# The second dense product of a retention and feed-forward kernel, from block 2 on, as Strassen's seven products of quarters

## The chip, the cores and the metric

One core of a Trainium2 chip. The metric is the device time of one execution, in microseconds. The kernel's engines are named as the profile names them: PE (TensorE), DVE (VectorE), ACT (ScalarE), POOL (GpSimd) and SP (SyncE, which issues most transfers here).

## The reference

Inputs are `q`, `k`, `v` of 4 batches x 8 heads x 768 steps x 64, `w_in` 512 x 2048, `w_out` 2048 x 512 and `alpha` of 2048, all float32. A retention recurrence gives 3072 rows of 512, and a feed-forward block with a leaky activation follows:

```python
for t in range(S):
    state = gamma[None, :, None, None] * state + np.einsum('bhd,bhe->bhde', k[:, :, t], v[:, :, t])
    y[:, :, t] = scale * np.einsum('bhd,bhde->bhe', q[:, :, t], state)
...
x = y.transpose(0, 2, 1, 3).reshape(B * S, H * D)        # 3072 x 512
h = x @ w_in                                             # 3072 x 2048
g = np.maximum(h, 0.0) + alpha * np.minimum(h, 0.0)
out = g @ w_out                                          # 3072 x 512
```

## The kernel before

The 3072 rows are worked in six blocks of 512 (`NBLK`, numbered 0 to 5). Everything that TensorE reads is float16, its sums are float32 in PSUM. Each block has three kinds of work.

**Retention.** A block's rows are four units of 128 steps (`u0` to `u0 + 3`). `load` (line 114) brings a unit's k, q and v in, on SP's queue. `prep` has GpSimd scale k, then q by a table (`scaled`, line 125, two operations), has SP issue a transposing transfer of both (line 146), and has GpSimd cast v (line 140). In pairs of units, `scores` (line 220) and `states` (line 180) are small matmuls of 64 x 64. VectorE then forms the running states (`sums`, lines 195 to 201, with one step on GpSimd, line 203) and masks the scores (`masked`, line 234). `outputs` (line 254) multiplies masked scores and states, and ScalarE copies the result to `xT` (line 302), which the next block's first dense product reads. The first two blocks do this in double units (names that begin with `u`, lines 317 to 520), which the change does not touch.

**First dense product, `ffn1`.** Sixteen tiles `ft` of 128 hidden columns, each 4 matmuls of 128 x 128 weights by 512 columns (line 538) into one of four PSUM banks (`tag="pb"`). ScalarE takes the rectified negative `hm` (line 547, three buffers), and VectorE joins both into the tile `gt[:, ft, :]` (line 548, one operand in SBUF, one in PSUM). `ffn1_half` (lines 569 to 583) does the same with 256 columns, for block 0 alone.

**Second dense product, `ffn2`.** For each of four row groups of 128, sixteen matmuls with a piece of `gt` as weights and 512 columns of `w_out` (line 607). ScalarE copies the bank to `os` (line 616) and issues its store (line 620).

The order is written out by hand: each engine works its instructions in the order in which the program issues them. The products are generators, and `tick(gen, m)` issues the next `m` of their matmuls, so that the retention's steps lie between them. In blocks 1 to 4 the next block's units run between the matmuls of the second product, and their scaling is issued within the first:

```python
gen = ffn2(n)
if more:
    for i in range(0, UB, 2):
        us = [u0 + i, u0 + i + 1]
        pq = scores(us)
        states(us)
        sums(us[0])
        masked(us, pq)
        sums(us[1])
        tick(gen, 22)
        outputs(us)
        tick(gen, 8)
```

The last block has no such units beside it.

Of the kernel before, what the change touches and what calls it, by code (L numbers as in the profile page):

```python
# [9 lines left out]
FP = mybir.dt.float32  # L10
F16 = mybir.dt.float16
COPY = mybir.ActivationFunctionType.Copy
RELU = mybir.ActivationFunctionType.Relu
MULT = mybir.AluOpType.mult
ADD = mybir.AluOpType.add


@with_exitstack
def kernel(
# [10 lines left out]
    nc = tc.nc  # L30
    B, H, S, D = q.shape
    d_model, d_ff = moe_w_in.shape
    NFT = d_ff // 128
# [4 lines left out]
    UB = 4  # L38
    NBLK = NU // UB
    TB = UB * C  # L40
    scale = 1.0 / np.sqrt(D)
# [63 lines left out]
    def load(u):  # L105
        b, c = divmod(u, NCH)
        kq_ = ring(f"kqs{u}")
        if u % 2 == 0:
            vpair[u] = vpair[u + 1] = ring(f"vs{u}")
        v_ = vpair.pop(u)[:, 512 * (u % 2) : 512 * (u % 2) + 512]  # L110
        t = {"k": kq_[:, 0:512], "q": kq_[:, 512:1024], "v": v_}
        for nm, src in (("k", k), ("q", q), ("v", v)):
            t[nm] = t[nm].rearrange("p (h d) -> p h d", d=D)
            nc.sync.dma_start(
                out=t[nm],
                in_=src[b, :, C * c : C * c + C, :].rearrange("h p d -> p h d"),
            )
        staged[u] = t
# [92 lines left out]
    def scores(us, again=0):  # L211
        sc = [ps("sca"), ps("scb")]
        for _ in range(again):
            nc.tensor.matmul(out=sc[0], lhsT=ident, rhs=wz, start=True, stop=True)
        for t, u in enumerate(us):
            for i in range(4):
                at = 64 * (4 * t + i)
                for r in range(2):
                    for X in range(2):
                        nc.tensor.matmul(  # L220
                            out=sc[r][HALF[X], at : at + 64],
                            lhsT=kqT[u][HALF[r], i, HALF[X]],
                            rhs=kqT[u][HALF[r], 4 + i, HALF[X]],
                            start=True,
                            stop=True,
                        )
        return sc

    def masked(us, sc):
        m2s[us[0]] = []  # L230
        n = 4 * len(us)
        for r in range(2):
            m2 = sbp.tile([128, 8, 64], F16, tag=f"m2{r}", bufs=2, name=f"m2{r}")
            nc.vector.tensor_tensor(
                out=m2[:, 0:n, :],
                in0=sc[r][:, 0 : 64 * n].rearrange("p (a j) -> p a j", j=64),
                in1=mask.unsqueeze(1).to_broadcast([128, n, 64]),
                op=MULT,
            )
            m2s[us[0]].append(m2)  # L240
# [287 lines left out]

    gts = {}

    def ffn1(n, lo=0):
        if n not in gts:
            gts[n] = sbp.tile([128, NFT, TB], F16, tag="gt", bufs=2, name=f"gt{n}")
        gt = gts[n]
        for ft in range(lo, NFT):
            hps = ps("hps", tag="pb")
            for hp in range(4):
                nc.tensor.matmul(  # L538
                    out=hps,
                    lhsT=w_in_all[:, hp, 128 * ft : 128 * ft + 128],  # L540
                    rhs=xT[n][:, :, hp, :],
                    start=(hp == 0),
                    stop=(hp == 3),
                )
                if hp == 3:
                    hm = sbp.tile([128, TB], FP, tag="hm", bufs=3, name="hm")
                    nc.scalar.activation(out=hm, in_=hps, func=RELU, bias=0.0, scale=-1.0)  # L547
                    nc.vector.scalar_tensor_tensor(  # L548
                        out=gt[:, ft, :],
                        in0=hm,  # L550
                        scalar=oma_sb[:, ft : ft + 1],
                        in1=hps,
                        op0=MULT,
                        op1=ADD,
                    )
                yield

    def ffn1_half(n, half, lo=0, hi=NFT, again=0, late=None):
        if n not in gts:
            gts[n] = sbp.tile([128, NFT, TB], F16, tag="gt", bufs=2, name=f"gt{n}")  # L560
        gt = gts[n]
        to = slice(256 * half, 256 * half + 256)
        for f0 in range(lo, hi, 2):
            hps = ps("hps", tag="pb")
            for _ in range(again if f0 == lo else 0):
                nc.tensor.matmul(out=hps, lhsT=ident, rhs=wz, start=True, stop=True)
            for ft in (f0, f0 + 1):
                for hp in range(4):
                    nc.tensor.matmul(  # L569
                        out=hps[:, 256 * (ft - f0) : 256 * (ft - f0) + 256],  # L570
                        lhsT=w_in_all[:, hp, 128 * ft : 128 * ft + 128],
                        rhs=xT[n][:, half, hp, :],
                        start=(hp == 0),
                        stop=(hp == 3),
                    )
                    if ft > f0 and hp == 3:
                        hm = sbp.tile([128, TB], FP, tag="hm", bufs=3, name="hm")
                        nc.scalar.activation(out=hm, in_=hps, func=RELU, bias=0.0, scale=-1.0)

                        def prelu(f0=f0, hm=hm, hps=hps):  # L580
                            for f in (f0, f0 + 1):
                                at = slice(256 * (f - f0), 256 * (f - f0) + 256)
                                nc.vector.scalar_tensor_tensor(  # L583
                                    out=gt[:, f, to],
                                    in0=hm[:, at],
                                    scalar=oma_sb[:, f : f + 1],
                                    in1=hps[:, at],
                                    op0=MULT,
                                    op1=ADD,
                                )  # L590

                        if late is None:
                            prelu()
                        else:
                            late.append(prelu)
                    yield

    def ffn2(n, parts=1):
        gt = gts.pop(n)
        opss = {}  # L600
        step = NFT // parts
        for f0 in range(0, NFT, step):
            for tq in range(UB):
                if f0 == 0:
                    opss[tq] = ps("ops", tag="pb")
                for ft in range(f0, f0 + step):
                    nc.tensor.matmul(  # L607
                        out=opss[tq],
                        lhsT=gt[:, ft, 128 * tq : 128 * tq + 128],
                        rhs=w_out_all[:, ft, :],  # L610
                        start=(ft == 0),
                        stop=(ft == NFT - 1),
                    )
                    if ft == NFT - 1:
                        os_sb = sbp.tile([128, d_model], FP, tag="os", bufs=4, name="os")
                        nc.scalar.activation(  # L616
                            out=os_sb, in_=opss[tq], func=COPY, bias=0.0, scale=1.0
                        )
                        row = TB * n + 128 * tq
                        (nc.scalar if n else nc.sync).dma_start(out=out[row : row + 128, :], in_=os_sb)  # L620
                    yield


    def flush(late):
        while late:
# [2 lines left out]
    def tick(gen, m):  # L628
        for _ in range(m):
            if next(gen, 1) == 1:  # L630
                return
# [171 lines left out]
    gen = ffn1(1)  # L803
# [7 lines left out]
    prep(11)  # L811
    load(14)
    load(15)
    for _ in gen:
        pass

    for n in range(1, NBLK):
        more = n + 1 < NBLK
        u0 = UB * (n + 1)
        if n > 1:  # L820
            gen = ffn1(n)
            if more:
                for i in range(UB):
                    tick(gen, 14)
                    prep(u0 + i)
                    if u0 + i + UB < NU:
                        load(u0 + i + UB)
            for _ in gen:
                pass
        gen = ffn2(n)  # L830
        if more:
            for i in range(0, UB, 2):
                us = [u0 + i, u0 + i + 1]
                pq = scores(us)
                states(us)
                sums(us[0])
                masked(us, pq)
                sums(us[1])
                tick(gen, 22)
                outputs(us)  # L840
                tick(gen, 8)
        for _ in gen:
            pass


# [28 lines left out]
```

## Time and profile before

| | |
|---|---|
| median of 3 runs | 214.5 us (214.11 to 214.72) |
| the profiled execution | 213.28 us, of which the span of the core's instructions is 211.5 us |
| busy in the span | PE 202.4, DVE 116.5, ACT 95.5, POOL 75.2 us |
| line 607 (second product) | 384 matmuls |
| line 538 (first product, whole blocks) | 352 matmuls |
| transfers | 27.44 MB read, 6.29 MB written |

How to read the rows that follow. In the groups by line, a row names line, engine, operation, output and inputs, the shape, how often it ran, then its busy time in us with the mean of one in ns, and behind the second bar the idle time of the engine just ahead of it with what ended most of it. In the timeline a row begins with the start and the length in us; equal instructions that follow each other are one row with their count. In the chain of waits, the work that ended last is followed back from the end; a row is start, length and the engine and line that held the chain. PE's matmuls are pipelined, so one's duration is longer than the distance between two; `PEclk` is the clock that was granted, in tenths.

### The profile page before, as it was taken

The page shows a single profiled execution, that of the slowest core. Times are in us where ns is not written, and L with a number is a line of the kernel's source. Part 1 is how long each engine was busy: PE and PEld are TensorE (multiplying, and loading weights), DVE is VectorE, ACT ScalarE, POOL GpSimd, SP SyncE. Part 2 cuts the span into 40 slices and gives each one's busy share as a digit, 9 for nine tenths or more (in the row PEclk, how much of TensorE's full clock was granted, in tenths as well). Part 3 has the DMA queues.
Part 4 walks back from the last instruction along what each step waited for, and adds up shares of the span by engine and source line. Part 5 has one row for each costly group of instructions (what it writes and reads, how often), then busy time and mean ns, then how long its engine had stood idle before and what let it go on. Part 6 is the DMA issues. An engine that isn't in the chain of part 4 may idle for free.

```text
span 211.5 us, 5579 instructions
## 1 busy us (share of the span) xinstructions
PE 202.4 (96%) x2355; PEld 100.6 (48%) x2355; DVE 116.5 (55%) x193; ACT 95.5 (45%) x160; POOL 75.2 (36%) x106
## 2 busy tenths in 40 slices
PE   7779999999999999999999999999999999999993
PEld 3544855454444554444454444444444444444441
DVE  2676997565288722288722388531488540588000
ACT  2334575353766232566233566133566133665121
POOL 0336899348830209900207930118920210000000
PEclk9999999999999999999999999999999999999999
DMA  6999999999999999999512999813660111100112
GB/s 181 332 333 359 394 376 337 319 297 218 249 271 241 193 262 212 276 219 224 134 53 99 237 203 226 194 52 113 159 69 0 52 55 50 50 3 0 50 70 79
DMA packets 87688, 38.27 MB, mean 181 GB/s; under 512 B 68064, under 2 KB 80496, under 8 KB 87664
## 3 DMA queue, kind: packets, MB, share of 16 engines
q1 hardware_dynamic: 84464, 32.60, 61.5%
q10 hardware_dynamic: 3200, 5.33, 7.0%
q8 instruction: 18, 0.29, 0.6%
q14 instruction: 6, 0.05, 0.1%
HBM read 27.44 MB, written 6.29 MB: 159 GB/s over the span
## 4 chain that ended last, share of the span: by engine, by line
PE 89%; DMA 5%; DVE 2%; issue 1%; SPq 1%; ACT 0%; DVEq 0%
PE ops L607 40%; PE hps L538 36%; DMA ku<-in_k_dram 3%; PE hps L569 3%; PE ya L254 2%; DMA qu<-in_q_dram 2%; DVE ukq L331 1%; PE sca L220 1%; PE trb L360 1%; PE ya L462 1%; PE sca L439 1%; PE yb L254 1%; SPq L317 1%; PE sta L180 1%; PE sta L374 1%
## 5 line engine op out<-in xcount | busy, mean ns | idle before, releaser
L548 DVE SCALAR_TENSOR_TENSOR gt<-hm,oma,hps 128x512 f16<-128x512 f32 x88 | 65.4, 747 | 42.9 <-ACT hm L547 33.9
L607 PE MATMUL ops<-wout,gt 128*128 128x512 f16 x384 | 87.7, 380 | 0.0
L538 PE MATMUL hps<-xT,win 128*128 128x512 f16 x352 | 77.0, 379 | 0.0
L547 ACT ACTIVATE hm<-hps 128x512 f32<-128x512 f32 x88 | 52.5, 597 | 23.5 <-PE hps L538 23.0
L607 PEld LDWEIGHTS <-gt 128*128 128x128 f16 x384 | 35.6, 98 | 40.4
L538 PEld LDWEIGHTS <-win 128*128 128x128 f16 x352 | 34.4, 98 | 41.4 <-issue 0.2
L616 ACT ACTIVATE os<-ops 128x512 f32<-128x512 f32 x24 | 14.3, 597 | 54.2 <-PE ops L607 54.1
L203 POOL TENSOR_TENSOR t<-ss,tab 128x256 f16<-128x256 f32 x13 | 8.0, 612 | 74.7 <-DVE ss L201 74.7
L125 POOL TENSOR_TENSOR kq<-kqs,tab 128x512 f16<-128x512 f32 x32 | 32.7, 1041 | 1.7 <-DMA kqs<-in_k_dram 1.7
L195 DVE TENSOR_TENSOR t<-t,sta 128x256 f16<-128x256 f16 x13 | 5.4, 412 | 14.5 <-PE stb L180 14.5
L673 POOL CAST wout<-wo 128x512 f16<-128x512 f32 x14 | 8.3, 613 | 6.7 <-DMA wo<-in_moe_w_out_dram 6.3
L302 ACT ACTIVATE xT<-ya 128x512 f16<-128x512 f32 x8 | 4.8, 597 | 11.6 <-PE yb L254 11.6
L140 POOL CAST vx<-vs 128x512 f16<-128x512 f32 x16 | 9.7, 609 | 0.0
L673 POOL CAST win<-wi 128x512 f16<-128x512 f32 x14 | 8.2, 613 | 3.0 <-DMA wi<-in_moe_w_in_dram 3.0
L369 ACT ACTIVATE ukT<-trb 128x512 f16<-128x512 f16 (+1 forms) x8 | 5.6, 704 | 6.7 <-PE trb L360 6.7
L569 PE MATMUL hps<-xT,win 128*128 128x256 f16 x64 | 7.5, 273 | 0.4 <-ACT xT L520 0.4
L450 DVE TENSOR_TENSOR um<-sca,mi 128x512 f16<-128x512 f32 x8 | 5.5, 687 | 3.5 <-PE scb L439 3.5
L569 PEld LDWEIGHTS <-win 128*128 128x128 f16 x64 | 6.1, 98 | 1.6 <-issue 0.8
L360 PE MATMUL trb<-mi,ukq 128*128 128x128 f16 x64 | 4.9, 220 | 1.8 <-DVE ukq L331 1.8
L346 POOL CAST uv<-vu 128x512 f16<-128x512 f32 x6 | 3.6, 612 | 8.3 <-DMA vu<-in_v_dram 8.2
L583 DVE SCALAR_TENSOR_TENSOR gt<-hm,oma,hps 128x256 f16<-128x256 f32 x16 | 6.3, 472 | 0.0
L201 DVE TENSOR_TENSOR ss<-t,stb 128x256 f32<-128x256 f16 x13 | 5.5, 421 | 1.0
(72 smaller groups left out, 145.3 us busy)
## 6 DMA issues: line engine op xcount, KB each, us to landing
out_dram<-os ACTq DMA_DIRECT2D x20, 256.0 KB, 2.0
wo<-in_moe_w_out_dram SPq DMA_DIRECT2D x8, 512.0 KB, 8.3
kqs<-in_k_dram SPq DMA_DIRECT2D x16, 256.0 KB, 3.9
kqs<-in_q_dram SPq DMA_DIRECT2D x16, 256.0 KB, 4.3
vs<-in_v_dram SPq DMA_DIRECT2D x16, 256.0 KB, 4.5
wi<-in_moe_w_in_dram SPq DMA_DIRECT2D x6, 512.0 KB, 7.7
ku<-in_k_dram SPq DMA_DIRECT2D x3, 512.0 KB, 7.2
vu<-in_v_dram SPq DMA_DIRECT2D x3, 512.0 KB, 7.6
```

Of the source, the lines that this page charges most:

```text
L125: eng.tensor_tensor(out=kqs[u][:, a].rearrange("p i r d -> p r i d"), in0=staged[u][nm].rearrange("p (r i) d -> p r i d", i=4), in1=tab[:, ...
L140: eng.tensor_copy(out=vs16[u], in_=staged[u]["v"])
L203: nc.gpsimd.tensor_tensor(out=t0, in0=ss, in1=tab[:, 2 * H : 2 * H + 4].unsqueeze(2).to_broadcast([128, 4, 64]), op=MULT,)
L254: ins = nc.tensor.matmul(out=yv[X][HALF[c], hp, t, :], lhsT=lhsT, rhs=rhs, start=(X, c) not in fresh, stop=last, skip_group_check=True,)
L360: nc.tensor.transpose(out=trv[:, i - i0, :, j, :], in_=ukq[w][:, a, j, i].rearrange("p r d -> p (r d)"), identity=ident,)
L538: nc.tensor.matmul(out=hps, lhsT=w_in_all[:, hp, 128 * ft : 128 * ft + 128], rhs=xT[n][:, :, hp, :], start=(hp == 0), stop=(hp == 3),)
L547: nc.scalar.activation(out=hm, in_=hps, func=RELU, bias=0.0, scale=-1.0)
L548: nc.vector.scalar_tensor_tensor(out=gt[:, ft, :], in0=hm, scalar=oma_sb[:, ft : ft + 1], in1=hps, op0=MULT, op1=ADD,)
L569: nc.tensor.matmul(out=hps[:, 256 * (ft - f0) : 256 * (ft - f0) + 256], lhsT=w_in_all[:, hp, 128 * ft : 128 * ft + 128], rhs=xT[n][:, half ...
L607: nc.tensor.matmul(out=opss[tq], lhsT=gt[:, ft, 128 * tq : 128 * tq + 128], rhs=w_out_all[:, ft, :], start=(ft == 0), stop=(ft == NFT - 1),)
L616: nc.scalar.activation(out=os_sb, in_=opss[tq], func=COPY, bias=0.0, scale=1.0)
L673: eng.tensor_copy(out=to, in_=t)
```

## The change

From block 2 on, the second product's operands are taken as 2 x 2 quarters: rows in two halves of 256, hidden columns in two halves of eight tiles (`HF`), output columns in two halves of 256. Instead of eight products of quarters there are seven, of sums of quarters, in the arrangement with shared sums.

- `w_sums` forms four sums of quarters of `w_out` (128 x 2048 each): two on GpSimd behind block 1's last `prep`, two on VectorE within block 1's second product.
- `g_sums` forms four sums of quarters of `gt`, each in two parts of 128 x 1024 (part 0: hidden tiles 0 to 3 and 8 to 11, part 1: the others). Sum 1 needs sum 0, and sum 3 needs sum 1. VectorE forms sums 0 and 1, GpSimd sums 2 and 3. The first parts of sums 0, 1 and 2 are issued within the first product, behind its tenth tile; on GpSimd that stands between the `prep` of the second and of the third unit. The others are issued at the end of the first product or, on GpSimd, between the steps of `sums`.
- `ffn1` takes its tiles in the order 0, 8, 1, 9, ..., 7, 15.
- `seven` issues 7 x 16 matmuls of 256 columns into four banks. Products that belong together add up in a bank; ScalarE copies a bank three times in between (`kept`), VectorE adds bank and copy to `os` (`put`, four times), and ScalarE issues the store of a quarter, 256 rows of 256 columns. The last quarter's store is issued behind two tiles of the next first product.
- Scores and states of the first pair of units now stand ahead of the last sums; `tick` counts are 40 and 16 instead of 22 and 8.
- `gt` has one buffer instead of two.

```diff
-    def ffn1(n, lo=0):
+    def ffn1(n, lo=0, fts=None):
...
-            gts[n] = sbp.tile([128, NFT, TB], F16, tag="gt", bufs=2, name=f"gt{n}")
+            gts[n] = sbp.tile([128, NFT, TB], F16, tag="gt", bufs=1, name=f"gt{n}")
...
-        for ft in range(lo, NFT):
+        for ft in fts or range(lo, NFT):
...
+    def minus(eng, out, a, b, op=SUB):
+        eng.tensor_tensor(out=out, in0=a, in1=b, op=op)
...
+        f = slice(4 * part, 4 * part + 4)
+        f8 = slice(HF + 4 * part, HF + 4 * part + 4)
+        t0, t1 = slice(0, 256), slice(256, 512)
+        if which == 0:
+            minus(eng, sm[0][:, f], gt[:, f, t1], gt[:, f8, t1], op=ADD)
+        elif which == 1:
+            minus(eng, sm[1][:, f], sm[0][:, f], gt[:, f, t0])
+        elif which == 2:
+            minus(eng, sm[2][:, f], gt[:, f, t0], gt[:, f, t1])
+        else:
+            minus(eng, sm[3][:, f], gt[:, f8, t0], sm[1][:, f])
...
+        def product(bank, a, w, first=False):
+            for t in range(2):
+                for f in range(HF):
+                    nc.tensor.matmul(
+                        out=bank[:, 256 * t : 256 * t + 256],
+                        lhsT=a[:, f, 128 * t : 128 * t + 128],
+                        rhs=w[:, f, :],
...
+        b, a = ps("ops", tag="pb"), ps("ops", tag="pb")
+        yield from product(b, A(0, 0), W(0, 0), True)
+        s1 = kept(b, "um0")
+        yield from product(a, A(0, 1), W(1, 0), True)
+        store = put(0, 0, a, s1)
+        yield from product(b, sm[1], wsum[1])
+        u2 = kept(b, "um0")
+        store()
+        c = ps("ops", tag="pb")
+        yield from product(c, sm[0], wsum[0], True)
+        yield from product(b, sm[2], wsum[2])
+        u3 = kept(b, "um1")
+        store = put(1, 1, c, u3)
+        d = ps("ops", tag="pb")
+        yield from product(d, A(1, 1), wsum[3], True)
+        store()
+        store = put(1, 0, u3, d, SUB)
+        yield from product(c, sm[3], W(1, 1))
+        store()
+        late_stores.append(put(0, 1, c, u2))
...
+            gen = ffn1(n, fts=[HF * (f % 2) + f // 2 for f in range(NFT)])
+            tick(gen, 8)
+            flush(late_stores)
+            tick(gen, 6)
+            for i in range(UB):
+                if more:
                     prep(u0 + i)
                     if u0 + i + UB < NU:
                         load(u0 + i + UB)
+                tick(gen, 14)
+                if i == 1:
+                    g_sums(n, 0, 0, nc.vector)
+                    g_sums(n, 0, 1, nc.vector)
+                    g_sums(n, 0, 2, nc.gpsimd)
...
+            if more:
+                us = [u0, u0 + 1]
+                pq = scores(us)
+                states(us)
+            g_sums(n, 1, 0, nc.vector)
+            g_sums(n, 1, 1, nc.vector)
+            pend = [(1, 2), (0, 3), (1, 3)]
...
+        pool_sum(1 if more else 3)
+        gen = seven(n) if quick else ffn2(n)
```

More of the change, by code (lines that the diff above doesn't have):

```diff
@@ L15 @@
 ADD = mybir.AluOpType.add
+SUB = mybir.AluOpType.subtract
 @with_exitstack
@@ L559, in ffn1_half @@
         if n not in gts:
-            gts[n] = sbp.tile([128, NFT, TB], F16, tag="gt", bufs=2, name=f"gt{n}")
+            gts[n] = sbp.tile([128, NFT, TB], F16, tag="gt", bufs=1, name=f"gt{n}")
         gt = gts[n]
@@ L621, in ffn2, with w_sums @@
                     yield
+    HF = NFT // 2
+    gsum, wsum = {}, {}
+    def minus(eng, out, a, b, op=SUB):
+        eng.tensor_tensor(out=out, in0=a, in1=b, op=op)
+    def w_sums(which, eng):
+        b = [[w_out_all[:, HF * j : HF * j + HF, 256 * l : 256 * l + 256] for l in range(2)] for j in range(2)]
+        i = which
+        wsum[i] = sbp.tile([128, HF, 256], F16, tag=("ukq", "ukT")[i // 2], bufs=2, name=f"wsum{i}")
+        x, y = (
+            (lambda: (b[0][1], b[0][0])),
+            (lambda: (b[1][1], wsum[0])),
+            (lambda: (b[1][1], b[0][1])),
+            (lambda: (wsum[1], b[1][0])),
+        )[i]()
+        minus(eng, wsum[i], x, y)
@@ new lines, in g_sums @@
+    def g_sums(n, part, which, eng):
+        if n not in gsum:
+            gsum[n] = [
+                sbp.tile([128, HF, 256], F16, tag=f"gs{i}", bufs=1, name=f"gs{n}{i}") for i in range(4)
+            ]
+        gt, sm = gts[n], gsum[n]
+        f = slice(4 * part, 4 * part + 4)
[9 more added lines that the diff above has]
+            minus(eng, sm[3][:, f], gt[:, f8, t0], sm[1][:, f])
@@ new lines, in seven, with A, W, kept @@
+    def seven(n):
+        gt, sm = gts.pop(n), gsum.pop(n)
+        def product(bank, a, w, first=False):
[5 more added lines that the diff above has]
+                        rhs=w[:, f, :],
+                        start=first and t == 0 and f == 0,
+                        stop=(f == HF - 1),
+                        skip_group_check=True,
+                    )
+                    yield
+        def A(i, j):
+            return gt[:, HF * j : HF * j + HF, 256 * i : 256 * i + 256]
+        def W(j, l):
+            return w_out_all[:, HF * j : HF * j + HF, 256 * l : 256 * l + 256]
+        def kept(bank, tag):
+            t = sbp.tile([128, 512], FP, tag=tag, bufs=2, name="kept")
+            nc.scalar.activation(out=t, in_=bank, func=COPY, bias=0.0, scale=1.0)
+            return t
+        def put(i, l, x, y, op=ADD):
+            os_sb = sbp.tile([128, d_model], FP, tag="os", bufs=4, name="os")
+            nc.vector.tensor_tensor(out=os_sb, in0=x, in1=y, op=op)
+            row = TB * n + 256 * i
+            return lambda: nc.scalar.dma_start(
+                out=out[row : row + 256, 256 * l : 256 * l + 256].rearrange(
+                    "(t p) c -> p t c", p=128
+                ),
+                in_=os_sb.rearrange("p (t c) -> p t c", t=2),
+            )
+        b, a = ps("ops", tag="pb"), ps("ops", tag="pb")
[18 more added lines that the diff above has]
+        late_stores.append(put(0, 1, c, u2))
@@ L624, in flush @@
+    late_stores = []
     def flush(late):
@@ L813 @@
     load(15)
+    w_sums(0, G)
+    w_sums(2, G)
     for _ in gen:
@@ L819 @@
         u0 = UB * (n + 1)
+        quick = n > 1
         if n > 1:
[L821 to L824, printed above, removed]
+            gen = ffn1(n, fts=[HF * (f % 2) + f // 2 for f in range(NFT)])
[4 more added lines that the diff above has]
+                if more:
                     prep(u0 + i)
@@ L827, with pool_sum @@
                         load(u0 + i + UB)
+                tick(gen, 14)
[3 more added lines that the diff above has]
+                    g_sums(n, 0, 2, nc.gpsimd)
             for _ in gen:
                 pass
-        gen = ffn2(n)
+        pend = []
+        if quick:
+            if more:
[5 more added lines that the diff above has]
+            pend = [(1, 2), (0, 3), (1, 3)]
+        def pool_sum(m=1):
+            for p, w in pend[:m]:
+                g_sums(n, p, w, nc.gpsimd)
+            del pend[:m]
+        pool_sum(1 if more else 3)
+        gen = seven(n) if quick else ffn2(n)
         if more:
@@ L833 @@
                 us = [u0 + i, u0 + i + 1]
-                pq = scores(us)
-                states(us)
+                if i or not quick:
+                    pq = scores(us)
+                    states(us)
                 sums(us[0])
+                pool_sum()
                 masked(us, pq)
                 sums(us[1])
-                tick(gen, 22)
+                pool_sum()
+                tick(gen, 40 if quick else 22)
+                if n == 1:
+                    w_sums(1 + i, nc.vector)
                 outputs(us)
-                tick(gen, 8)
+                tick(gen, 16 if quick else 8)
         for _ in gen:
             pass
+    flush(late_stores)
 _INS = ['q', 'k', 'v', 'moe_w_in', 'moe_w_out', 'moe_alpha']
```

## The prediction

> **What bounds the kernel now.** I read the page's busy line and clock row first, then the chain of waits, then the timeline of one block.
>
> ```profile
> PE 202.4 (96%) x2355; PEld 100.6 (48%) x2355; DVE 116.5 (55%) x193; ACT 95.5 (45%) x160; POOL 75.2 (36%) x106
> PEclk9999999999999999999999999999999999999999
> PE 89%; DMA 5%; DVE 2%; issue 1%; SPq 1%; ACT 0%; DVEq 0%
> ```
> ```profile
> 22.42 5.35 PE hps L569 x48
> ...
> 117.75 13.81 PE hps L538 x64
> 131.56 0.15 PE sca L220 x2
> 132.21 4.86 PE ops L607 x22
> ...
> 149.00 13.81 PE hps L538 x64
> ...
> 194.04 13.83 PE ops L607 x64
> 207.89 0.60 ACT os L616
> ```
>
> From block 2 on TensorE never waits: 64 matmuls of 512 columns take 13.81 us in the first product and 13.83 in the second, 216 ns each at full clock, and a block takes 149.00 - 117.75 = 31.25 us. So a matmul saved is time saved, and any wait put ahead of TensorE is time added.
>
> **The products.** Per block 64 matmuls of 512 columns (13.83 us) become 7 x 16 = 112 of 256 columns. The only such matmuls before are line 569's.
>
> ```profile
> 22.35 5.42 PE L569 MATMUL hps<-xT,win 128*128 128x256 f16 x48
> ```
>
> The last one's pipelined 0.27 us taken off, (5.42 - 0.27)/47 = 109.5 ns each, so 112 x 0.1095 = 12.27: 1.56 us saved per block. The chain's 5.35/48 = 111.5 ns would leave 1.35; both loaded new weights for every matmul, as the seven products do. A page of the Trainium skill speaks against the change here: "TensorE: Matmul & The Clock Gate", section Back-to-back issue gap, gives sustained spacings of about 81 ns at 128 columns and 131 ns at 512. A straight line between them, my estimate, is 98 ns at 256, and 112 x 0.098 - 64 x 0.131 would be 2.6 us lost per block. The rows above disagree (216 and 109.5 ns), so it gets no chance.
>
> **What the sums cost alone.** A part of a sum is 128x1024, all 16-bit and in SBUF. Before has no such VectorE operation; the nearest rows:
>
> ```profile
> L548 DVE SCALAR_TENSOR_TENSOR gt<-hm,oma,hps 128x512 f16<-128x512 f32 x88 | 65.4, 747 | 42.9 <-ACT hm L547 33.9
> L234 DVE TENSOR_TENSOR m<-sca,mi 128x512 f16<-128x512 f32 x8 | 5.5, 683 | 0.0
> L367 DVE COPY ukT<-trb 128x512 f16<-128x512 f16 x6 | 2.5, 423 | 3.4 <-PE trb L360 3.4
> L201 DVE TENSOR_TENSOR ss<-t,stb 128x256 f32<-128x256 f16 x13 | 5.5, 421 | 1.0
> L125 POOL TENSOR_TENSOR kq<-kqs,tab 128x512 f16<-128x512 f32 x32 | 32.7, 1041 | 1.7 <-DMA kqs<-in_k_dram 1.7
> L203 POOL TENSOR_TENSOR t<-ss,tab 128x256 f16<-128x256 f32 x13 | 8.0, 612 | 74.7 <-DVE ss L201 74.7
> ```
>
> Lines 201 and 234 give (683 - 421)/256 = 1.02 ns per element, so 683 + 512 x 1.02 = 1.2 us at worst. The all-16-bit copy does 512 in 423 ns, about half per element: 0.423 + 512 x 0.52 ns = 0.69 us. I take 0.69, since every operand is 16-bit as in the copy, and keep 1.2. GpSimd: lines 203 and 125 give 1.68 ns per element, so 1.9 us a part.
>
> The weights' sums (twice the size: two on GpSimd, 1.04 + 1536 x 1.68 ns = 3.6 us each, two on VectorE in block 1) cost nothing: GpSimd has 11.04 us idle ahead of block 1's second product, and VectorE waits out the rest of its stage.
>
> ```profile
> 71.23 0.61 POOL L203 TENSOR_TENSOR t<-ss,tab 128x256 f16<-128x256 f32 x1 [11.04 <-DVE ss L201]
> ```
>
> **What the sums cost together.** VectorE and GpSimd work at the same time with two SBUF inputs each only once before:
>
> ```profile
> 15.16 0.68 DVE L331 TENSOR_TENSOR ukq<-qu,tab 128x512 f16<-128x512 f32 x1
> 15.33 0.99 POOL L413 TENSOR_TENSOR ut<-uss,tab 128x256 f16<-128x256 f32 x1 [3.27 <-DVE uss L411]
> 15.77 1.10 DVE L331 TENSOR_TENSOR ukq<-qu,tab 128x512 f16<-128x512 f32 x1
> ```
> ```profile
> L413 POOL TENSOR_TENSOR ut<-uss,tab x3: 612/613/991, 15.3 to 50.8; 128x256 f16<-128x256 f32 x3
> ```
>
> GpSimd's operation takes 0.99 instead of 0.61: it runs after VectorE's first has ended (15.84). VectorE's second takes 1.10 instead of 0.68: it ends 0.55 us after GpSimd's end (16.32). They take turns, whole operations at a time; line 548 (one SBUF tensor, one PSUM) keeps its 0.75 beside a busy GpSimd. The Trainium skill, "SBUF — State Buffer", section SBUF: two separate sides, states this as a rule: a VectorE operation with two SBUF inputs and a GpSimd one exclude each other for a whole instruction, and who starts first holds. By that rule, the trace agrees; without turns the sum would be that of the first rival. Bounds for a wait of VectorE: 0, or the rest of a GpSimd operation (up to 1.04 us behind line 125, 1.9 behind a part of a sum). I take turns.
>
> **First half of the sums, inside the first product.** Times count from its first matmul, 117.59.
>
> ```profile
> 117.59 13.98 PE L538 MATMUL hps<-xT,win 128*128 128x512 f16 x64
> 118.86 1.26 ACT L547 ACTIVATE hm<-hps 128x512 f32<-128x512 f32 x2 [0.47 <-PE hps L538]
> 119.49 13.49 DVE L548 SCALAR_TENSOR_TENSOR gt<-hm,oma,hps 128x512 f16<-128x512 f32 x16 [7.15 <-ACT hm L547]
> 129.68 1.89 PE L538 MATMUL hps<-xT,win 128*128 128x512 f16 x8
> 23.08 6.34 DVE L583 SCALAR_TENSOR_TENSOR gt<-hm,oma,hps 128x256 f16<-128x256 f32 x16
> L583 DVE SCALAR_TENSOR_TENSOR gt<-hm,oma,hps 128x256 f16<-128x256 f32 x16 | 6.3, 472 | 0.0
> ```
>
> Tile i (0 to 15) of gt starts on VectorE at 1.90 + 0.863 i and takes 0.75; without a wait VectorE does one each 0.67 us (line 583's sixteen: (6.34 - 0.47)/15 = 0.39, that is 0.08 under one's duration). GpSimd, queued between the units' scalings, does sum 2 when tile 6 is there, 7.9 to 9.8, then unit u0+2's k (to 10.84) and q. VectorE's sum 0 is due behind tile 9, at 10.34: it waits for k, ends 11.4. q was waiting and holds to 12.4; sum 1, which needs sum 0, ends 12.9. Tile 10 then starts at 12.9 instead of 10.53 and ends 13.65. Tile 14's matmuls, due at 129.68 - 117.59 = 12.09, write the PSUM bank that tile 10 empties (four banks in turn), and start at 13.7: **1.6 us lost**. SP's order is unchanged, but its last two transposes of units follow GpSimd some 6 us later; they are needed some 5 us after they land, so nothing is lost.
>
> **Second half, at the seam.** Tile 14: matmul 13.7, ScalarE 14.97 to 15.57, gt at 16.35; tile 15 ends 17.2. GpSimd's sum 2, freed by tile 14, holds 16.4 to 18.3. VectorE's sum 0 is due at 17.1, ends 18.85; sum 1 ends 19.65. Queued behind them are the state sums and masks, for which the unit's outputs wait:
>
> ```profile
> 132.90 0.41 DVE L195 TENSOR_TENSOR t<-t,sta 128x256 f16<-128x256 f16 x1
> 133.41 0.42 DVE L201 TENSOR_TENSOR ss<-t,stb 128x256 f32<-128x256 f16 x1
> 133.75 0.68 DVE L234 TENSOR_TENSOR m<-sca,mi 128x512 f16<-128x512 f32 x1
> 134.35 0.68 DVE L234 TENSOR_TENSOR m<-scb,mi 128x512 f16<-128x512 f32 x1
> 134.95 0.41 DVE L195 TENSOR_TENSOR t<-t,sta 128x256 f16<-128x256 f16 x1
> 136.99 0.22 PE L254 MATMUL ya<-m,vx 64*64 64x64 f16 x2
> 137.26 0.20 PE L254 MATMUL ya<-kt,t 64*64 64x64 f16 x2
> ```
>
> Before, they end 135.36, 1.9 us ahead of their last use (137.26). Now they take the same 2.46 us from 19.6: 22.05. TensorE ends the first product at 15.4, scores and states take 0.65, and 40 matmuls of 109.5 ns bring the outputs to 20.45 and that last use to 20.7: **1.4 us lost**. The second pair of units, with nothing beside it, waits for nothing. A middle block (2, 3, 4): -1.56 + 1.6 + 1.4 = +1.44; three: +4.3.
>
> **Last block.** No scalings, so sum 0 and 1 run 10.34 to 11.8, tile 10 ends 12.5: 0.45 lost. No scores either: product 1 starts at 14.26 and its eighth matmul (15.03) waits for tile 14 (15.2): 0.25. GpSimd's sum 2 holds 15.25 to 17.15, VectorE's sum 0 then ends 17.7, GpSimd's waiting sum 3 holds to 19.6, sum 1 ends 20.15; product 3's fifth matmul, due at 18.45, needs it: 1.75. Product 7 waits for copy and addition behind product 5, about 0.1. Together -1.56 + 2.55 = +1.0.
>
> **Stores.**
>
> ```profile
> 207.89 0.60 ACT L616 ACTIVATE os<-ops 128x512 f32<-128x512 f32 x1 [2.86 <-PE ops L607]
> 208.52 0.34 ACTq L620 DMA_DIRECT2D out_dram<-os  x1
> out_dram<-os ACTq DMA_DIRECT2D x20, 256.0 KB, 2.0
> kqs<-in_k_dram SPq DMA_DIRECT2D x16, 256.0 KB, 3.9
> ```
>
> As many stores, in 1 KB rows instead of 2 KB; only the last shows. An addition (line 234's 0.68) replaces a copy of 0.60, and ScalarE's queue must hear of it: +0.2. Landing lies between 2.0 and the 3.9 of the 256-byte loads, so 0 to 1.9 more; I take 0, nearer to the store.
>
> **Sum.** 4.3 + 1.0 + 0.2 = +5.5. The profiled execution took 213.28 (span 211.5 and 1.8 around it): 218.8. The runs' median, 214.5, is 1.2 above it: **220.0 us**.
>
> **Rivals.**
> - *The engines don't take turns* (the one overlap is special: line 413's first call). Then a middle block loses 0.45 in the first product, as the last block does, and about 0.35 at the outputs: -0.76. The last: -0.76. Sum 4 x -0.76 + 0.2 = -2.8: **211.6**. For it: one event only. Against: both sides of it fit turns to 0.1 us.
> - *Turns in one place only*, for instance GpSimd reaches unit u0+2 later than tile 9 or gives way faster: 3 x 1.2 less than forecast and below, **213 to 217**.
> - *Sums at 1.2 us.* Half a microsecond more in each of four steps in a row: a middle block loses 2.7 + 2.4, the last 4.7: 3 x 3.5 + 3.1 + 0.2 = +13.8: **228**. For it: no two-input 16-bit row in before; against: line 367.
> - *GpSimd keeps its turn* from one operation to the next: sum 0 waits for the whole of both scalings, to 15.1, and tile 10 starts near 16.5, 6 us late: about +5 a block, **231**. In the one event the waiting engine got its turn.
>
> It decides between signs at 1.56 us of waits per block.
>
> **Chances.** Forecast 0.55 (217 to 222.5), no turns 0.22, turns in one place 0.10, slow sums 0.09, GpSimd keeping 0.04. A measurement of this kernel can tell about 0.3% (0.6 us) from no change. Faster: 0.22 + 0.03; same 0.03; slower 0.72. The range from 210.5 to 225 takes in the no-turns case and leaves out the last two and a little below, under 0.2.
>
> **What would show it.** Products at 109 to 112 ns in the chain of waits. GpSimd's line-125 operations and sums well above 1.04 and 1.9 us where VectorE's sums run, and VectorE's sums at 1.1 to 2 us instead of 0.69. A gap on TensorE of 1.6 us before tile 14 in blocks 2 to 4 released by VectorE, another of 1.4 before the first outputs, and one of 1.75 in the last block's product 3. If VectorE's sums all take 0.69 the forecast is wrong and the first rival right.

## The result, and the profile after

The changed kernel takes 220.62 us (median, 219.9 to 221.44) where the kernel before, run beside it, takes 214.61: a ratio of 1.0284, with a 95% interval of 1.0234 to 1.0334. The forecast was 220.0 from 214.5. The profiled execution is the fastest of these runs, 219.9. A ratio leaves out runs in a slower state of the chip and is not formed from the medians, so here and below it can differ by some 0.2% from theirs.

The page of the changed kernel: span, busy times, granted clock and the chain's shares by engine. The lines of before are moved by one (its line 125 is 126 here); line 632 is now a sum, 670 a product's matmul, 688 `kept`, 693 `put`, 695 the store of a quarter.

```profile
span 218.1 us, 6015 instructions
PE 197.8 (91%) x2547; PEld 119.2 (55%) x2547; DVE 149.2 (68%) x227; ACT 92.5 (42%) x156; POOL 122.0 (56%) x124
PEclk9999999999999999999999999999999999999999
PE 53%; DVE 24%; DMA 13%; POOL 3%; issue 2%; SPq 2%; ACT 1%; ACTq 0%; DVEq 0%; POOLq 0%
```

TensorE works 4.6 us less at an unchanged clock, and the chain, once 2% VectorE, is now 24% VectorE. Where that sits shows in a table of stretches, cut at the first matmul of blocks 2, 3, 4 and of the last. Columns: stretch, its length, then each engine's busy time with its number of instructions (PE, weight loads, VectorE, ScalarE, GpSimd), granted clock, DMA share, GB/s. Before:

```profile
86.32:117.59 31.27, 31.03 (x378) 14.80 (x376) 17.35 (x28) 14.11 (x24) 10.51 (x14) 1.00 0.69 160
117.59:148.84 31.25, 31.00 (x378) 14.77 (x377) 16.93 (x27) 14.11 (x24) 12.09 (x17) 1.00 0.75 170
148.84:180.07 31.23, 31.01 (x386) 14.77 (x385) 16.92 (x27) 14.11 (x24) 7.55 (x11) 1.00 0.26 61
```

After:

```profile
87.20:119.51 32.31, 29.89 (x426) 19.61 (x425) 24.14 (x35) 14.00 (x24) 20.09 (x18) 1.00 0.73 141
119.51:153.22 33.71, 30.06 (x427) 19.61 (x424) 24.36 (x35) 13.09 (x23) 21.44 (x20) 1.00 0.76 158
153.22:185.59 32.37, 29.86 (x434) 19.56 (x432) 24.59 (x35) 13.41 (x23) 18.05 (x16) 1.00 0.25 68
```

Before, TensorE idles 0.2 us in a block. After, it works some 1.1 us less and idles 2.4 to 2.5 us in blocks 2 and 4, 3.65 in block 3. No other engine is busy for more than 0.76 of a block, so the time is in waits. The blocks grow by 1.04, 2.46 and 1.14 us, the last block by 0.84 (27.79 to 28.63, up to its last matmul), the tail by 0.24 (3.64 to 3.88); block 1 is 0.14 shorter. That is 5.6 us. The rest of the spans' 6.6 lies ahead of block 1's first product (54.91 to 55.93) and does not come from the change (the run of before once more, below).

The sums of the changed kernel by tile (shortest, median and longest, in ns):

```profile
L632 DVE TENSOR_TENSOR gs<-gt x8: 682/1738/1999, 97.3 to 201.2; 128x1024 f16<-128x1024 f16 x8
L632 DVE TENSOR_TENSOR gs<-gs,gt x8: 691/1054/2489, 98.6 to 203.2; 128x1024 f16<-128x1024 f16 x8
L632 POOL TENSOR_TENSOR gs<-gt x8: 2121/2125/2127, 94.9 to 200.5; 128x1024 f16<-128x1024 f16 x8
```

VectorE's part takes 0.68 us when nothing is in its way and up to 2.49 when GpSimd is. The timeline of block 2, whose first matmul is at 87.20, shows the two stalls:

```profile
87.20 12.25 PE L539 MATMUL hps<-xT,win 128*128 128x512 f16 x56
94.91 2.13 POOL L632 TENSOR_TENSOR gs<-gt 128x1024 f16<-128x1024 f16 x1 [8.18 <-DVE gt L549]
96.99 2.49 POOL L126 TENSOR_TENSOR kq<-kqs,tab 128x512 f16<-128x512 f32 x2
97.33 1.25 DVE L632 TENSOR_TENSOR gs<-gt 128x1024 f16<-128x1024 f16 x1
98.62 1.42 DVE L632 TENSOR_TENSOR gs<-gs,gt 128x1024 f16<-128x1024 f16 x1
99.43 1.07 POOL L141 CAST vx<-vs 128x512 f16<-128x512 f32 x1
99.95 4.09 DVE L549 SCALAR_TENSOR_TENSOR gt<-hm,oma,hps 128x512 f16<-128x512 f32 x6
100.74 1.89 PE L539 MATMUL hps<-xT,win 128*128 128x512 f16 x8 [1.29 <-DVE gt L549]
103.40 2.12 POOL L632 TENSOR_TENSOR gs<-gt 128x1024 f16<-128x1024 f16 x1 [0.34 <-DVE gt L549]
104.08 2.00 DVE L632 TENSOR_TENSOR gs<-gt 128x1024 f16<-128x1024 f16 x1
106.11 0.69 DVE L632 TENSOR_TENSOR gs<-gs,gt 128x1024 f16<-128x1024 f16 x1
108.32 0.22 PE L255 MATMUL ya<-m,vx 64*64 64x64 f16 x2 [0.55 <-DVE m L235]
108.92 0.22 PE L255 MATMUL yb<-m,vx 64*64 64x64 f16 x2 [0.38 <-DVE m L235]
```

The first stall: sum 0 waits for the end of k's scaling, q's scaling then has its turn, sum 1 follows, and GpSimd's cast waits for that (1.07 instead of 0.60). Tile 10 starts 12.75 us after the block's first matmul, and TensorE idles 1.29 us ahead of tile 14. The second: sum 0 waits for GpSimd's sum 2, and the masks behind it come late for the outputs. In the last block sum 0 and sum 1 each wait for a sum of GpSimd's, and product 3 waits for sum 1:

```profile
201.18 2.00 DVE L632 TENSOR_TENSOR gs<-gt 128x1024 f16<-128x1024 f16 x1
203.21 2.49 DVE L632 TENSOR_TENSOR gs<-gs,gt 128x1024 f16<-128x1024 f16 x1
205.75 4.98 PE L670 MATMUL ops<-wsum,gs 128*128 128x256 f16 x44 [1.94 <-DVE gs L632]
```

Block 3 has a stall that was not forecast:

```profile
123.96 0.39 ACTq L695 DMA_DIRECT2D out_dram<-os  x1
124.46 2.07 ACT L548 ACTIVATE hm<-hps 128x512 f32<-128x512 f32 x4 [2.37 <-PE hps L539]
125.89 2.32 PE L539 MATMUL hps<-xT,win 128*128 128x512 f16 x10 [1.04 <-DVE gt L549]
```

The last quarter's store stands on ScalarE's queue behind two rectifications, the second of which ends at 122.09. It is issued at 123.96, although VectorE had finished what it stores at 120.40 (119.71 and 0.69). The chain of waits names what held it; the first row, from the timeline, is what came just ahead on GpSimd:

```profile
115.65 0.61 POOL L204 TENSOR_TENSOR t<-ss,tab 128x256 f16<-128x256 f32 x1 [1.39 <-DVE ss L202]
116.22 2.04 POOL kq L126 x2
118.29 5.60 DMA kt<-kq
123.96 0.39 ACTq L695
```

That is the transposing transfer of the first unit that is scaled for block 3's first product, 5.60 us from issue to landing. GpSimd's sums do not make it late: the last one of block 2 ended at 113.08 (110.96 and 2.12), and GpSimd then waited for VectorE's state steps. The scaling begins 3.29 us ahead of block 3's first matmul, and just as much in the run without sums below (114.48 and 117.77); before the change it began 4.51 us ahead (113.08 and 117.59). Why the store waits for this transfer stands in the trace's own records: both count their completion on the same semaphore, number 104, and ScalarE waits for that semaphore right ahead of the store. The rectifications of the next tiles are queued behind the store.

### The profile page after: what moved, and what is told of

Same layout as the page of the kernel before. It is cut to its first block, busy times and chain, and to the rows that moved or that the text cites. A ratio compares the mean times of both kernels' runs of the same rounds, so it can differ in the third digit from the quotient of the medians.

```text
span 218.1 us, 6015 instructions
## 1 busy us (share of the span) xinstructions
PE 197.8 (91%) x2547; PEld 119.2 (55%) x2547; DVE 149.2 (68%) x227; ACT 92.5 (42%) x156; POOL 122.0 (56%) x124
## 4 chain that ended last, share of the span: by engine, by line
PE 53%; DVE 24%; DMA 13%; POOL 3%; issue 2%; SPq 2%; ACT 1%; ACTq 0%; DVEq 0%; POOLq 0%
PE hps L539 20%; PE ops L608 12%; PE ops L670 12%; DVE gs L632 9%; DVE gt L549 9%; DMA ku<-in_k_dram 6%; DMA qu<-in_q_dram 4%; DMA kt<-kq 3%; DVE m L235 2%; POOL ukq L332 2%; PE ya L255 2%; ACT hm L548 1%; SPq L763 1%; PE yb L255 1%; PE trb L361 1%
## 5 line engine op out<-in xcount | busy, mean ns | idle before, releaser
L632 POOL TENSOR_TENSOR gs<-gt 128x1024 f16<-128x1024 f16 x8 | 17.0, 2125 | 40.5 <-DVE gt L549 33.3
L608 PE MATMUL ops<-wout,gt 128*128 128x512 f16 x128 | 30.2, 380 | 0.0
L670 PEld LDWEIGHTS <-gs 128*128 128x128 f16 x256 | 24.2, 98 | 5.3 <-DVE gs L632 2.2
L670 PE MATMUL ops<-wsum,gs 128*128 128x256 f16 x192 | 22.8, 273 | 1.9 <-DVE gs L632 1.9
L688 ACT ACTIVATE kept<-ops 128x512 f32<-128x512 f32 x12 | 7.2, 598 | 25.9 <-PE ops L670 25.9
L693 DVE TENSOR_TENSOR os<-ops,kept 128x512 f32<-128x512 f32 x12 | 8.3, 688 | 13.9 <-PE ops L670 7.3
L632 POOL TENSOR_TENSOR gs<-gt,gs 128x1024 f16<-128x1024 f16 x8 | 17.4, 2182 | 0.6 <-DVE gs L632 0.6
L670 PE MATMUL ops<-wout,gt 128*128 128x256 f16 x128 | 14.8, 273 | 0.0
L632 DVE TENSOR_TENSOR gs<-gt 128x1024 f16<-128x1024 f16 x8 | 12.7, 1593 | 0.1
L617 ACT ACTIVATE os<-ops 128x512 f32<-128x512 f32 x8 | 4.8, 597 | 12.8 <-PE ops L608 12.6
```

What stands on the lines that cost most here:

```text
L608: nc.tensor.matmul(out=opss[tq], lhsT=gt[:, ft, 128 * tq : 128 * tq + 128], rhs=w_out_all[:, ft, :], start=(ft == 0), stop=(ft == NFT - 1),)
L632: eng.tensor_tensor(out=out, in0=a, in1=b, op=op)
L670: nc.tensor.matmul(out=bank[:, 256 * t : 256 * t + 256], lhsT=a[:, f, 128 * t : 128 * t + 128], rhs=w[:, f, :], start=first and t == 0 and ...
L688: nc.scalar.activation(out=t, in_=bank, func=COPY, bias=0.0, scale=1.0)
L693: nc.vector.tensor_tensor(out=os_sb, in0=x, in1=y, op=op)
```

## The experiments

The theory: TensorE loses time only where VectorE's sums take turns with GpSimd's work, at three places, and in block 3 behind the late store. The main rivals: VectorE's own additional work delays the tiles, turns or no turns; or seven products of quarters save less than the row of line 569 says.

**Two engines by themselves.** A kernel of its own, with none of the reference's work: eight operations on VectorE and eight on GpSimd, alone and side by side, in one execution.

```python
def vsum():   # 8 x V.tensor_tensor(vo, va, vb, ADD)      128x1024, all 16-bit in SBUF
def vone():   # 8 x V.tensor_tensor(vo, bank, va, MULT)   128x512, one operand in PSUM
def gsum():   # 8 x G.tensor_tensor(go, ga, gb, ADD)      128x1024, all 16-bit in SBUF
def gscale(): # 8 x G.tensor_tensor(go, gf, gs.broadcast, MULT)   128x512
def gcast():  # 8 x G.tensor_copy(go, gf)                 128x512
```

> A kernel of its own that computes nothing of the reference: stages of 8 operations each, VectorE's 16-bit sum of 128x1024 alone, GpSimd's sum alone, GpSimd's scaling (128x512 float32 by a column) alone, then VectorE's sums beside GpSimd's sums, beside its scalings, beside its float32 casts, and last VectorE operations with one operand in PSUM beside GpSimd's sums. Theory (turns of whole operations): alone 0.69 and 2.12 us; together VectorE's take 2.1 to 2.8 us each beside sums (they alternate), 1.0 to 1.7 beside scalings, 0.6 to 1.3 beside casts, and the PSUM form keeps 0.68 beside GpSimd's sums, which keep 2.12. Rival (they share the port's bandwidth): both grow by the same share, VectorE's to about 1.0 and GpSimd's to about 2.6. Rival (no contention in general): all as alone.

The timeline rows: VectorE's sums alone, GpSimd's sums alone, its scalings alone; then VectorE's sums beside GpSimd's sums, scalings and casts; then VectorE with a PSUM operand beside GpSimd's sums.

```profile
23.85 4.94 DVE L58 TENSOR_TENSOR vo<-va,vb 128x1024 f16<-128x1024 f16 x8
30.03 16.61 POOL L66 TENSOR_TENSOR go<-ga,gb 128x1024 f16<-128x1024 f16 x8
47.93 8.04 POOL L70 TENSOR_TENSOR go<-gf,gs 128x512 f16<-128x512 f32 x8
56.91 16.46 DVE L58 TENSOR_TENSOR vo<-va,vb 128x1024 f16<-128x1024 f16 x8
57.66 19.75 POOL L66 TENSOR_TENSOR go<-ga,gb 128x1024 f16<-128x1024 f16 x8
78.34 10.02 DVE L58 TENSOR_TENSOR vo<-va,vb 128x1024 f16<-128x1024 f16 x8
79.21 11.05 POOL L70 TENSOR_TENSOR go<-gf,gs 128x512 f16<-128x512 f32 x8
91.20 7.42 DVE L58 TENSOR_TENSOR vo<-va,vb 128x1024 f16<-128x1024 f16 x8
92.05 7.59 POOL L79 CAST go<-gf 128x512 f16<-128x512 f32 x8
100.46 4.86 DVE L62 TENSOR_TENSOR vo<-bank,va 128x512 f16<-128x512 f32 x8
100.81 16.63 POOL L66 TENSOR_TENSOR go<-ga,gb 128x1024 f16<-128x1024 f16 x8
```

Side by side the two sets of sums last from 56.91 to 77.41, 20.50 us; one after the other they would be 4.94 + 16.61 = 21.55. Nearly nothing overlaps. VectorE gets two operations done first; from there each of its operations takes 2.6 us and each of GpSimd's 2.5 (alone 0.62 and 2.08 on average), so the waiting engine gets the next turn. VectorE's eighth ends at 73.37, with two of GpSimd's still to come. One grows fourfold and the other by a fifth, so they do not share in equal parts. With scalings it is 11.92 of 12.98. An operand in PSUM ends it: VectorE's 4.86 lie wholly within GpSimd's 16.63. The rule of the Trainium skill that the prediction drew on ("SBUF — State Buffer", section SBUF: two separate sides) agrees with these rows; that the engines alternate is what the rows add.

**GpSimd's first part behind all four scalings.** This takes the turns out of the first product alone.

```diff
-                    g_sums(n, 0, 2, nc.gpsimd)     # within the loop, i == 1
+            g_sums(n, 0, 2, nc.gpsimd)             # behind the loop
```

> Only GpSimd's first sum part of each block moves, behind the scalings of all four units; every operation stays on its engine, and nothing is left out. Theory (VectorE's and GpSimd's two-input operations take turns): GpSimd stands idle when VectorE's first two sum parts are due, so they take 0.69 us each instead of 1.25 to 1.48, and TensorE's stall ahead of tile 14 falls from 1.5 to about 0.45 us in blocks 2, 3 and 4: three times 1.05, so 220.6 goes to about 217.4 us. The seam stays as it is (second part of sum 0 still 2.0 us). Rival (VectorE simply has more work than its slack): its work is the same, so 220.6 stays.

Measured: 216.99 us beside 215.08, a ratio of 1.0069 (1.0023 to 1.0115). From its timeline, block 2:

```profile
88.65 14.14 PE L539 MATMUL hps<-xT,win 128*128 128x512 f16 x64
98.78 0.68 DVE L632 TENSOR_TENSOR gs<-gt 128x1024 f16<-128x1024 f16 x1
```

The first sum falls to 0.68 us (the second, just behind it, to 0.69), and the 64 matmuls run as one piece of 14.14, 0.16 over the 13.98 of before. The second stall stays: sum 0 takes 1.99 us there. VectorE has the same work as in the changed kernel, so its own work accounts for no more than the 0.16. Blocks 2 to 4 fall to 31.03, 31.60 and 30.99: 1.28, 2.11 and 1.38 less. Block 3 stays 0.6 above its neighbours.

**The seam and the last block apart.** The seam is where the first product passes into the second. GpSimd's second parts go behind the first state step; in the last block VectorE does the rest of the sums.

```diff
-                g_sums(n, p, w, nc.gpsimd)
+                g_sums(n, p, w, nc.gpsimd if more else nc.vector)
...
-        pool_sum(1 if more else 3)
+        pool_sum(0 if more else 3)
```

> Only the second sum parts move. In blocks 2 to 4 GpSimd takes them behind the first state step, so that VectorE's two parts come first; in the last block VectorE takes all five remaining parts itself. Nothing is left out. Theory (turns): VectorE's parts at the seam take 0.69 us each instead of 2.0 and 0.69, the wait of the outputs falls by about 1.3 us in three blocks, and the last block's wait in product 3 (1.9 us) goes: 3 x 1.3 + 1.9, so about 214.8 us. Rival (VectorE's own work is the bound): the last block gets slower by three parts, about 2 us, and the others stay: 221 to 222.

Measured: 214.08 us beside 215.08, 0.9971 (0.9934 to 1.0008), not to be told from the kernel before. The timeline has the first product's turns as they were (1.25 us for sum 0) and the seam's gone:

```profile
104.48 0.69 DVE L632 TENSOR_TENSOR gs<-gt 128x1024 f16<-128x1024 f16 x1
...
199.20 1.29 DVE L632 TENSOR_TENSOR gs<-gt,gs 128x1024 f16<-128x1024 f16 x2
```

Blocks 2 and 4 take 31.09 and 31.18, 1.2 less than in the changed kernel, block 3 31.81, and the last block 26.52 instead of 28.63. There VectorE alone is done with all of the last sums sooner than the two engines together were.

**Both.** The two edits above in one kernel.

> Both moves of the two runs before together; nothing is left out. Theory (turns): about 3.2 us from the first and 5.8 from the second, so 211.6 to 212, faster than before the change by about 1%; VectorE's sums all near 0.69 us. Rival (VectorE's work): 220 or more.

Measured: 210.7 us beside 215.08, 0.9789 (0.9718 to 0.986): faster than both kernels. Blocks 2 to 4 take 29.84, 30.61 and 29.80, the last 26.52. By its tiles:

```profile
L632 DVE TENSOR_TENSOR gs<-gt x9: 684/684/693, 97.8 to 194.8; 128x1024 f16<-128x1024 f16 x9
L632 DVE TENSOR_TENSOR gs<-gs,gt x8: 691/692/693, 98.5 to 194.2; 128x1024 f16<-128x1024 f16 x8
```

No sum of VectorE's waits any more. Block 3 alone is 0.8 longer than its neighbours.

**The late store.** In the changed kernel, with the store behind ten tiles of the next first product instead of two.

```diff
-            tick(gen, 8)
-            flush(late_stores)
-            tick(gen, 6)
+            tick(gen, 14)
...
                 if i == 1:
+                    flush(late_stores)
```

> Only the last quarter's store moves: it is issued behind ten tiles of the next first product instead of two. Theory: in block 3 that store waits on ScalarE's queue for the landing of a transposing transfer that counts on the same completion counter, and holds up the third rectification by 1.9 us, which costs block 3 about 1.4 us: 220.6 goes to about 219.2, block 3 as long as block 4 (32.4 us). Rival (block 3 is held by something else, such as late data): 220.6 stays.

Measured: 219.93 us beside 215.08, 1.0228 (1.0159 to 1.0297), against 1.0284 for the changed kernel; these intervals overlap. The blocks tell it apart: block 3 falls from 33.71 to 32.36, and blocks 2 and 4 stay at 32.30 and 32.38. Block 3, in the columns of the tables above:

```profile
120.07:152.43 32.36, 29.89 (x426) 19.64 (x424) 24.59 (x35) 13.42 (x23) 21.45 (x20) 1.00 0.79 165
```

The store has another semaphore here (107) than the transfer (104).

**No sums.** The seven products take plain quarters instead of sums of quarters, and no sum is formed; the rest of the schedule stands.

```diff
-        yield from product(b, sm[1], wsum[1])
+        yield from product(b, A(1, 0), W(0, 1))
...                                    # likewise the four others with sums
```

> All sums of quarters are left out, of the weights and of the first product's result: the seven products take plain quarters of equal size instead, so the result is another one. All 112 matmuls, copies, additions and stores stay. Both theories (the sums cost, not the products): 1.56 us saved per block and no stall, four times, and 0.2 more at the end: 214.6 - 6.0 = about 208.5 us. Rival (256-column products with new weights cost more than half, or bank copies hold them up): 211 or more.

Measured: 210.13 us beside 216.12, 0.974 (0.9668 to 0.9811). Block 2:

```profile
88.09:117.77 29.68, 29.44 (x426) 19.50 (x425) 19.42 (x31) 14.00 (x24) 9.42 (x13) 1.00 0.71 156
```

Block 4 takes 29.63: seven products save 1.59 to 1.60 us a block when nothing waits. Block 3 keeps 0.7 more, with the store where the change puts it and on the transfer's semaphore. The time lies between the 208.5 of the theory and the 211 of the rival. In the profiled execution, 0.7 us of that are in block 3 and 0.6 in block 1 (31.88 us, 31.27 in the changed kernel), ahead of the first of the seven products, so it does not speak for the rival.

**All three edits, and the sums spread.** The two regroupings with the later store; and the same with VectorE's first part moved up behind the ninth tile and its second behind the eleventh.

```diff
-                    g_sums(n, 0, 0, nc.vector)     # i == 1, both behind the tenth tile
-                    g_sums(n, 0, 1, nc.vector)
+                # sum 0 behind the ninth tile, sum 1 behind the eleventh
```

> Both regroupings of the turns together (GpSimd's first part behind the four scalings, its second parts behind the first state step, the last block's remaining parts all on VectorE), and the last quarter's store behind ten tiles as in e4. If block 3's stall comes from that store waiting behind an unrelated transposition, block 3 falls from the 30.61 us of e3_both_apart to the 29.8 of blocks 2 and 4, and the whole to about 0.977 of the kernel before (about 0.8 us less than e3_both_apart). Rival: with GpSimd's order changed the transposition lands in time, and block 3's 0.8 us more have another cause: block 3 stays at 30.6 and the ratio at 0.979.

> As e5_all_three, and VectorE's two parts in a first product go behind different tiles (the first two tiles earlier than the pair stood, the second where it stood). If the 0.16 us that a block still loses in its first product is VectorE's two parts back to back (1.38 us in one piece) ahead of a tile that PE waits for, it goes, and blocks 2 to 4 take about 29.65 instead of 29.8: 0.5 us less than e5_all_three in all. Rival: the idle is not from the pair but from VectorE's total (it cannot catch up): the same as e5_all_three.

Measured: 210.52 us, 0.9793 (0.9751 to 0.9834), and 210.11 us, 0.977 (0.972 to 0.9821), beside 214.66. Neither can be told from the 0.9789 above. Block 3 of the first:

```profile
118.67:148.55 29.88, 29.63 (x426) 19.50 (x424) 21.91 (x35) 13.41 (x23) 20.48 (x20) 1.00 0.87 179
```

Block 3 is level with its neighbours (29.84 and 29.80), so its extra time was the store's wait. The 0.7 us don't show in the run's time, whose interval is about as wide; in this profile they are hidden by block 1, which the edit does not reach and which took 31.80, its scores waiting for a transposing transfer. Spreading the sums was expected to save 0.5 us. Blocks 2 to 4 take 29.77, 29.80 and 29.82, which is 0.13 in all. Its timeline in block 4 shows a turn in the place of the pair:

```profile
156.07 2.12 POOL L632 TENSOR_TENSOR gs<-gt 128x1024 f16<-128x1024 f16 x1 [0.26 <-DVE gt L549]
157.54 1.20 DVE L632 TENSOR_TENSOR gs<-gt 128x1024 f16<-128x1024 f16 x1
```

The earlier sum met GpSimd's and waited 0.5 us. The edit also differs from the expectation, which has the first part two tiles earlier and the second where it stood: here they stand one tile earlier and one tile later. Whether a spread without turns helps stays open.

**Before once more.**

> The kernel before, unchanged, profiled once more. Block 1's first product began at 54.91 us in its first profile and at 55.93 in that of the changed kernel. If the start varies from run to run with the first loads, it comes here anywhere in 55 to 57.5 with blocks of 31.25 us, and the 1.0 us of the comparison is no cost of the change. Rival: the start is fixed for a program: 54.9 again, and the 1.0 us is a cost of the change that nothing in the changed lines explains.

It took 216.26 us (span 214.5). From its timeline:

```profile
57.91 13.97 PE L538 MATMUL hps<-xT,win 128*128 128x512 f16 x64
```

Block 1's first product starts 3.0 us later than in the first profile of the same kernel, and from there to the end both take 156.6 us. The start varies from one execution to the next, so the 1.0 us between the two profiles is no cost of the change.

## Why the prediction was right

- **Products.** 1.56 us saved per block; 1.59 to 1.60 measured without sums.
- **A part of a sum alone.** VectorE 0.69 as taken, which leaves out the rival of slow sums. GpSimd 2.12 instead of 1.9.
- **Turns.** As taken, and GpSimd does not keep its turn. They decide the sign: 1.028 with them, 0.979 with both places mended. With one place mended the runs took 216.99 and 214.08 us, within the 213 to 217 of the rival of turns in one place only.
- **First half.** The working had sum 0 end 11.4 us after the block's first matmul, sum 1 at 12.9 and tile 10 start at 12.9. The trace has 11.38, 12.84 and 12.75. TensorE's wait was 1.29 in block 2 where 1.6 was forecast.
- **Second half.** Sum 0 due at 17.1 and ended at 18.85 in the working; 16.88 and 18.88 in the trace. The outputs lost 1.2, by what block 2 gained with the seam apart, where 1.4 was forecast, and the second pair lost nothing, as said.
- **Blocks 2 and 4** therefore grew by 1.04 and 1.14 where 1.44 was forecast.
- **Last block.** The wait in product 3 was 1.94 (forecast 1.75), the block +0.84 (forecast +1.0).
- **Tail.** +0.24 (forecast +0.2).
- **The step that failed** is the price of the stores, of which "only the last shows", and with it the sum that takes the three middle blocks as alike. The store that stands behind two tiles of block 3's first product waited for a transposing transfer on the same semaphore, and that cost 1.35 us in that block. What the prediction says of a block's last two transposing transfers held: they came later, and no unit waited for them.

The sum, +5.5 forecast and +5.6 measured from block 1's first product on, is nearer than its parts, and that is luck. The turns in the middle blocks cost 1.0 us less than worked out, and the late store 1.35 more. The medians lie 6.0 apart. Of the chances, the 0.22 for no turns had one event for it and the fit of both its sides against it; that fit was the better evidence.

The price of the rival without turns was mis-sized too. It gave -2.8, by 0.45 lost within the first product and 0.35 at the outputs. With the turns taken away, VectorE's own additional work costs 0.16 in the first product (14.14 against 13.98) and nothing at the outputs. Such a kernel gains some 4 us.

## What to carry to other kernels

Of the forms that were run side by side here, only the one with an input in PSUM let VectorE and GpSimd work at the same time; while VectorE reads two tiles in SBUF, add the times of both engines, and put GpSimd's share beside VectorE's PSUM work. In an order written out by hand, moving one instruction past a few others can be worth more than the arithmetic saved: here some 10 us lie between the same sums in two orders (and, in the last block, on one engine instead of two). Where an order is changed, follow the transfers too, to everything that waits on the same semaphore, on other queues as well.

## What the runs showed of the hardware

- GpSimd's cast, with one input in SBUF, takes turns with VectorE's sums as well: 1.07 us instead of 0.60 in block 2, and eight beside eight of VectorE's sums took 7.59 and 7.42 us. The prediction counted only GpSimd operations with two inputs; the Trainium skill, "SBUF — State Buffer", section SBUF: two separate sides, says of any GpSimd instruction that reads SBUF that it contends. These rows agree.
- A store's issue waited for a transposing transfer on another queue that it has no data in common with: its data was ready at 120.40, the transfer landed at 123.89, and the issue came at 123.96. Both are on semaphore 104. So they are in the five profiles in which block 3 is 0.6 to 1.4 us longer than its neighbours (the changed kernel, the two single regroupings, both, and no sums). In the three with the later store the numbers differ, and block 3 is level; so they do for block 4's store in the changed kernel, which went out at 155.28, as soon as ScalarE had taken up the rectification ahead of it (155.21).
- GpSimd's 16-bit sums are dearer than the line through its rows of before: 2.12 us instead of 1.9 for 128x1024, and 4.08 instead of 3.6 for a weights' sum of 128x2048. The Trainium skill, "GPSIMD Engine Reference", section 2.1 Instruction dispatch, gives about 2.5 cycles per element as a floor for two inputs, which at the 1.2 GHz of its section 1 is an estimate of 2.13 us for the first, as measured, and of 4.27 for the second, where 4.08 was measured; the measurement decides.
